# Modulation products by channel columns, and loads in another order, in a one-core mixer kernel

## The chip, the cores and the metric

The kernel runs on one core of a Trainium2 chip. A time is the device time of one launch in microseconds. The profiles show the engines of that core: PE (matrix products; PEld is its weight load), DVE, ACT and POOL (elementwise work), and SP, whose queue issues nearly all DMA transfers.

## The reference, cut to what matters

S = 2048 tokens, D = 640 channels, F = 1728; all in float32.

```python
mod = (silu(c) @ w_mod).reshape(1, 6, 1, D)         # w_mod: 640 x 3840
sa, ca, ga, sb, cb, gb = mod[:, 0], ..., mod[:, 5]
h = layernorm(x) * (1 + ca) + sa                    # x is q
x = x + ga * A(h, k, v, shift_k, ssm_k, ssm_D)
h = layernorm(x) * (1 + cb) + sb
x = x + gb * mixer_mlp(h, w1, b1, w2, b2)

def A(q, k, v, ...):
    kv = causal_conv_of_4_taps(k, shift_k) * v
    y = irfft(rfft(kv, 2 * S) * rfft(ssm_k, 2 * S))[:S] + kv * ssm_D
    return q * y                                    # per channel
```

## The kernel before

The operator A runs in five stages of 128 channels (the loop `for c in range(NC)`); a token MLP follows it. In a stage the long convolution is two small Fourier steps forward, a product, and two back:

- `step1(side, t)` is the first step, on PE, in four blocks t of 16 products; side 0 is kv (tile `X`, read with a stride), side 1 is ssm_k (tile `P`). ACT evacuates each block into `Z` (line 232).
- `f2(g)`, g = 0 to 7, is the second step (line 246), with the weights `W2`. ACT evacuates half of it to `KT` (line 250), DVE makes two products into `P` (`mul`), POOL adds them into `Y`, the tile `T_y` (`add`).
- `i2(r)`, r = 0 and 1, is the first step back (line 275, evacuated at 283 into part of `Z`), `i1(half)` the second (line 294, weights `V1`, the inverse's constant `c_v1`).
- `gate(c, ps, half)`: DVE multiplies by A1, the normalised and scaled q, and POOL adds to x. A1 is made by sixteen ACT operations `ac` (line 301, they need the statistics of the rows of q) and by DVE's scalings `po` with the rows G1 and G0.

The loop is software-pipelined. While stage c runs f2, i2 and i1, `step1` of stage c + 1 is woven in, and DVE fills its gaps (`dv(n)` takes n operations from the list `fill`) with the short convolution `kv_ops` of the stage after that, eight operations for each of four groups of rows. Group 2 is done by POOL for stages 0, 1 and 2. `kv_loads` and `load_k`, `load_v`, `load_halo` bring K and V in pieces of 128 KB, each issued on SP as soon as its group's last reader is issued.

Engines take their instructions in the order in which the program gives them (`manual_schedule`), so the order of the statements is the order on each engine and on SP's queue. A transfer waits on SP for the readers of the place that it overwrites, and all later transfers wait behind it; it also waits for the eighth transfer before it. Three PSUM buffers go around for PE's results (`psum`); the fourth, `tap`, holds DVE's kv work (`SV`, `TAP`).

What the change touches, in the order of time:

- The weights W2 are laid out by ACT: `lay_w2(i, n)` (line 110) copies quarter n of half i from a load `load_w2c(i)` in the tile `xb`. Half 0 is loaded before stage 1's K and V (line 481), half 1 behind them (489). The four lays of half 0 stand between the blocks of `step1(0, t)` of stage 0.
- q is loaded in 32 transfers (`load_q`, at f2's g = 3), into `xa` and `xb`, the second where the halves of W2 came in. Behind it come w_mod's blocks of 128 rows and 1920 columns, five of them (`mod_load`), into `T_v1`, `T_aux` and `P`.
- Statistics of q: DVE's `bn_stats` after f2 of stage 0 (lines 561, 562). `rstd` makes the reciprocal root from them: a root on ACT (338), an addition on POOL (339), four operations of DVE.
- Modulation of the first half of `mod`: `mod_part` (line 354) multiplies silu(c) with a block of w_mod, five parts of six products of 320 columns; `mod_sum` (358) evacuates; `mod_row(i)` (365) spreads row i over the partitions, and ACT and DVE make G0 and G1 of all 640 columns (372 to 377). They stand around `i2` of stage 0.
- The inverse's constant lands in `T_v1` where two w_mod blocks were, so it waits for `mod_part` 0 and 1. `load_ks(1)`, ssm_k of stage 1, lands in the first half of `T_aux` and waits for `mod_part` 2. Then come stage 2's K and V.
- `perm_add` and `perm` (line 176) bring ssm_k into `P`, which `step1(1, t)` reads behind i1.

Of the kernel before, what the change touches and what calls it, by code (L numbers as in the profile page):

```python
# [50 lines left out]
def mixer_kernel(ctx: ExitStack, tc: tile.TileContext, q, k, v, shift_k, ssm_k, ssm_D, w1, b1, w2, b2, c,  # L51
# [129 lines left out]

        act.activation(TAP, TR.rearrange("p (i s) -> p s i", s=4), AF.Copy)

    def kv_ops(g, eng=dve):
        S_, T_, W_ = (SV, TV, TAP) if eng is dve else (PS_.rearrange("p (n i) -> p n i", i=64),
                                                       PT.rearrange("p (n i) -> p n i", i=64), PW)
        w = lambda s: W_[:, None, s, :].to_broadcast([128, 8, 64])
        kx = lambda s: KX[:, 8 * g + 3 - s:8 * g + 11 - s, :]
        ops = [lambda: TT(eng, S_, kx(3), w(3), ALU.mult)]
        for s in (2, 1, 0):  # L190
            ops.append(lambda s=s: TT(eng, T_, kx(s), w(s), ALU.mult))
            ops.append(lambda: TT(eng, S_, S_, T_, ALU.add))
        ops.append(lambda: TT(eng, X.rearrange("p (n i) -> p n i", i=64)[:, 8 * g:8 * g + 8], S_,
                              VX[:, 8 * g:8 * g + 8], ALU.mult))
        return ops

# [22 lines left out]
        return ops  # L219


    def step1(side, t, later=False):

        ps = psum()
        for a in range(8):
            i = 8 * t + a
            lhs = KSP[:, i] if side else X.rearrange("p (m i) -> p i m", i=32)[:, i]
            o = 512 * (a % 2) + 128 * (a // 2)
            for ri in range(2):
                pe.matmul(ps[64 * ri:64 * ri + 64, o:o + 128], lhs, F1[:, 128 * ri:128 * ri + 128], start=True,  # L230
                          stop=True)
        evac = lambda: act.activation(Z[:, side, t].rearrange("p a k e -> p e a k"),  # L232
                                      ps.rearrange("p (e a k) -> p e a k", a=8, e=2), AF.Copy)
        return evac if later else evac()
# [126 lines left out]
    def mod_row(i, t, slot=None, later=False):  # L361

        ps, j = psum(slot).rearrange("p (h m) -> p h m", h=2), i % 3
        for h in range(2):
            pe.matmul(ps[:, h, 0:320], ones[32 * j:32 * j + 1, 0:1].to_broadcast([1, 128]),
                      t[32 * j:32 * j + 1, 320 * h:320 * h + 320], start=True, stop=True)
# [4 lines left out]
        if i == 0:  # L371
            act.activation(two(G0), ps, AF.Copy)
        elif i == 1:
            act.activation(two(G1), ps, AF.Copy, bias=1.0)
        elif i == 2:
            TT(dve, two(G0), ps, two(G0), ALU.mult)
            TT(dve, two(G1), ps, two(G1), ALU.mult)
        elif i == 3:
            act.activation(two(SB), ps, AF.Copy, accum_out=msb)
        elif i == 4:  # L380
            dve.tensor_scalar(two(CB), ps, 1.0, None, op0=ALU.add)


    NF, NW = 14, 2
    FS = (4, 5, 6, 7, 8, 9, 10, 11, 12)
# [87 lines left out]
    def run(ops):  # L473
        for f_ in ops:
            f_()
# [1 line left out]

    all_taps()
    load_taps(1, act)
    run(kv_ops(2, pool))  # L480
    load_w2c(0)
    run(kv_ops(0))
    kv_loads(1, 0)
    run(kv_ops(1))
    kv_loads(1, 1)
    kv_loads(1, 2)
    run(kv_ops(3))
    kv_loads(1, 3)
    load_w2c(1)
    for h in range(2):  # L490
        sync.dma_start(stg[7 * h:7 * h + 6, :], dram(b1, 864 * h, [[128, 6], [1, 128]]))
# [3 lines left out]
    perm_add(0)  # L495
    perm(0)
    all_taps()
    load_taps(2)
    for t in range(4):
        step1(0, t)  # L500
        lay_w2(0, t)
    run(kv_ops(2, pool))
    run(kv_ops(0))
    run(kv_ops(1))
    for t in range(4):
        step1(1, t)


    three = lambda t: [t[:, 640 * j:640 * j + 640] for j in range(3)]
    pl = [three(t) for t in (T_v1, T_v1[:, 1920:3840], T_aux, T_aux[:, 2048:3968], P)]  # L510

    def load_q():
        for j in range(16):
            for b in range(2):
                sync.dma_start(XH[j // 8][64 * b:64 * b + 64, j % 8], dram(q, (16 * b + j) * D, [[32 * D, 64], [1, D]]))
        for kk in range(4):
            mod_load(0, kk, (T_v1[:, 0:1920], T_v1[:, 1920:3840], T_aux[:, 0:1920], T_aux[:, 2048:3968])[kk])

    fill = kv_ops(3)

# [5 lines left out]
    for c in range(NC):  # L526
# [3 lines left out]
        for g in range(8):  # L530
            m_, a_ = f2(g)
            if pend_m:
                pend_m()
            if pend_a:
                pend_a()
            pend_a, pend_m = (pend_m and pa_next), m_
            pa_next = a_
            if c:
                for f_ in ac[2 * g:2 * g + 2]:
                    f_()  # L540
            if cn is None and g < 4:
# [23 lines left out]
            if c + 3 < NC:  # L565
                load_taps(c + 3)
        if c == 0:
            mod_load(0, 4, P[:, 0:1920])
            for t in range(4):
                step1(0, t)  # L570
            ps = psum()
            pe.transpose(ps[:, 0:36], stg, ID[0:36, 0:36])
            act.activation(cols, ps[:, 0:36], AF.Copy)
            act.activation(sil, cols[:, 30:35], AF.Silu)
            i2(0)
            for kk in range(4):
                mod_part(tap, kk, pl[kk])
                if kk == 1:
                    sync.dma_start(T_v1[:, 0:4096], c_v1, max_dma_last_dim=4096)
                if kk == 2:  # L580
                    load_ks(1)
            rstd(rs1, nm1, 0, 16)
            run(ac[0:4])
            i2(1)
            mod_part(tap, 4, pl[4])
# [12 lines left out]
            run(kv_ops(2, pool))  # L598
            for i in range(3):
                mod_row(i, T_kt[:, 0:640])  # L600
            taps()
            load_taps(3)
            perm_add(1, dve)
            perm(1)
            load_ks(2)
            run(ac[8:16])
            run(po[0:2])
            fill.extend(kv(3, ((0,), (1, 2), (3,))))
        elif cn is not None:
            for t in range(2):  # L610
                step1(0, t)
            perm(cn)
            if c + 2 < NC:
                fill.extend(kv(c + 3 if c + 3 < NC else None))
            else:
                fill.extend(x1s(cc, j) for cc in range(c) for j in range(16))
        else:
            blk.update({f: (j16(t[:, 0:2048]), j16(t[:, 2048:4096])) for f, t in (
                (0, mem("w0", 4096, "wb0")), (1, mem("w1", 4096, "wb1")))})
            mod_load(3, 3, T_z[:, 0:1920])  # L620
            mod_load(3, 4, P[:, 0:1920])
            for kk in range(3):
                mod_part(tap, kk, pl[kk])
            t = mem("in", 4288, "wb3")
            blk[3] = j16(t[:, 0:2048]), j16(t[:, 2048:4096])
            split_rows(0, X, (0, 1, 3))
            split_rows(1, T_aux[:, 0:2048], (0, 1, 3))
            run(po)
        if c:
# [25 lines left out]
        for half in range(2):  # L655
            ps = i1(half)
            if c and half:
                dv(3)
            elif c:
                k0 = step1(1, 0, True)  # L660
            elif half:
                run(po[2:4])
# [534 lines left out]
```

## Time and profile before

| | us |
|---|---|
| median of 3 runs | 704.31 (702.51 to 707.6) |
| the profiled execution | 706.67 |
| its span, first to last instruction | 704.6 |
| PE busy / weight load busy | 641.4 / 620.4 |
| DVE busy | 501.5 |
| ACT busy | 307.8 |
| POOL busy | 156.1 |

The busy shares are sums over stages with different limits. In the five stages PE, DVE and POOL hand work to each other, and a stage is read by which of them ends a wait last; the MLP after them is PE's. The rows that matter stand in the prediction. A timeline row gives start and duration in us, engine and line, tiles, and in brackets how long the engine was idle before and what ended it. A row of windows gives, behind each engine's busy time, PE's granted clock, the share of the DMA engines and GB/s.

### The profile page before, as it was taken

What the parts mean: (1) busy time and instruction counts of PE and PEld (TensorE: products, weight loads), DVE (VectorE), ACT (ScalarE), POOL (GpSimd) and SP (SyncE); (2) the same over time, 40 slices, a digit from 0 to 9 for tenths busy, and PEclk for the clock granted to TensorE, in tenths of its full rate; (3) what the DMA queues carried; (4) which work ended last, traced back from release to release, by engine and by line L of the source; (5) the groups of instructions that cost most, each with busy time, mean ns of one, the idle gap of its engine ahead of it and who ended that gap; (6) DMA issues with size and microseconds to landing.
All of it is one profiled execution on the core that took longest, in us unless ns stands there. A gap on an engine that the chain in (4) does not pass through costs nothing.

```text
span 704.6 us, 20705 instructions
## 1 busy us (share of the span) xinstructions
PE 641.4 (91%) x9078; PEld 620.4 (88%) x9078; DVE 501.5 (71%) x846; ACT 307.8 (44%) x463; POOL 156.1 (22%) x135
## 2 busy tenths in 40 slices
PE   0699769999999999978888999999999999999997
PEld 0699569989989989758878999999999999999997
DVE  7688578969878638679886430564377699888886
ACT  0664644635745545345766420431243332333331
POOL 5297058625527328100010000000000000000000
PEclk9999979999999899799999999999999999999999
DMA  9978978346433522334030833357385634555511
GB/s 182 213 217 263 325 159 176 86 78 143 78 68 92 151 56 70 114 83 98 1 60 22 158 62 59 78 130 160 112 234 152 205 116 128 153 170 171 155 52 39
DMA packets 170848, 89.36 MB, mean 127 GB/s; under 512 B 89571, under 2 KB 160518, under 8 KB 170758
## 3 DMA queue, kind: packets, MB, share of 16 engines
q1 hardware_dynamic: 166210, 86.73, 48.8%
q10 hardware_dynamic: 4548, 1.31, 1.1%
q8 instruction: 71, 1.16, 0.7%
q14 instruction: 19, 0.16, 0.1%
HBM read 74.25 MB, written 13.76 MB: 125 GB/s over the span
## 4 chain that ended last, share of the span: by engine, by line
PE 67%; DVE 14%; DMA 6%; POOL 5%; ACT 4%; issue 3%; SPq 0%; ACTq 0%; DVEq 0%; POOLq 0%
PE pst L1059 20%; PE pst L446 17%; PE pst L246 8%; PE pst L230 7%; PE pst L275 6%; POOL y L60 4%; PE pst L1123 4%; PE pst L947 3%; DMA aux<-in_A_ssm_k_dram 3%; PE pst L294 2%; DVE aux L60 2%; DVE tap L60 1%; DVE p L60 1%; PE tap L354 1%; DVE kt L60 1%
## 5 line engine op out<-in xcount | busy, mean ns | idle before, releaser
L246 PEld LDWEIGHTS pst<-z,w 128*64 128x64 f32 x2560 | 94.7, 141 | 7.7 <-ACT z L232 7.3
L246 PE MATMUL pst<-z,w 128*64 128x64 f32 x2560 | 95.7, 240 | 6.2 <-ACT z L232 6.1
L60 POOL TENSOR_TENSOR y<-p 128x256 f32<-128x256 f32 x72 | 92.5, 1353 | 24.3 <-DVE p L60 23.9
L60 DVE TENSOR_TENSOR p<-pst,kt 128x512 f32<-128x512 f32 x80 | 52.6, 693 | 22.1 <-ACT kt L250 15.9
L230 PE MATMUL pst<-v,x 128*64 128x128 f32 x640 | 45.8, 304 | 23.2 <-POOL t L471 23.2
L232 ACT ACTIVATE z<-pst 128x1024 f32<-128x1024 f32 x40 | 45.8, 1144 | 43.9 <-PE pst L230 25.9
L230 PEld LDWEIGHTS pst<-v,x 128*64 128x64 f32 x640 | 43.8, 221 | 23.7 <-issue 23.2
L1059 PE MATMUL pst<-r_z,m_w 128*128 128x320 f32 x259 | 48.5, 309 | 1.3 <-DVE m_w L60 1.3
L275 PEld LDWEIGHTS pst<-v,y 32*128 32x128 f32 x1280 | 43.3, 210 | 6.5 <-POOL y L60 2.7
L275 PE MATMUL pst<-v,y 32*128 32x64 f32 x1280 | 45.3, 297 | 2.8 <-DVE y L60 2.1
L1047 ACT ACTIVATE m_w<-m_v 128x896 fp32r<-128x896 f32 x30 | 27.8, 948 | 42.6 <-DVE m_v L60 27.4
L230 PE MATMUL pst<-v,p 128*64 128x128 f32 x640 | 40.0, 284 | 7.0 <-DVE aux L60 4.9
L250 ACT ACTIVATE kt<-pst 128x512 f32<-128x512 f32 x40 | 25.2, 631 | 48.0 <-PE pst L246 25.6
L230 PEld LDWEIGHTS pst<-v,p 128*64 128x64 f32 x640 | 37.4, 143 | 8.3 <-DVE aux L60 5.1
L1059 PEld LDWEIGHTS pst<-r_z,m_w 128*128 128x128 f32 x259 | 40.6, 188 | 1.5 <-DVE m_w L60 1.5
L60 DVE TENSOR_TENSOR m_w<-m_v,m_w 128x896 fp32r<-128x896 f32 x30 | 32.5, 1087 | 11.2 <-ACT m_w L1047 11.2
L853 ACT ACTIVATE pst<-pst,sm 128x640 f32<-128x640 f32 x14 | 10.7, 767 | 59.3 <-PE pst L446 59.3
L60 DVE TENSOR_TENSOR tap<-tap,kt 128x512 f32<-128x512 f32 x51 | 35.6, 698 | 1.3
L60 DVE TENSOR_TENSOR kt<-in,tap 128x512 f32<-128x512 f32 x51 | 35.1, 688 | 1.5
L1059 PE MATMUL pst<-h_x,m_w 128*128 128x320 f32 x168 | 33.7, 309 | 0.0
L283 ACT ACTIVATE z<-pst 128x512 f32<-128x512 f32 x38 | 21.4, 665 | 27.9 <-PE pst L275 27.9
L1047 ACT ACTIVATE m_w<-m_p 128x896 fp32r<-128x896 f32 x13 | 12.4, 954 | 44.5 <-DVE m_p L60 27.6
(310 smaller groups left out, 1395.6 us busy)
## 6 DMA issues: line engine op xcount, KB each, us to landing
x<-in_B_w_dram SPq DMA_DIRECT2D x20, 512.0 KB
m_v<-in_B_w_dram SPq DMA_DIRECT2D x19, 384.0 KB
aux<-in_A_ssm_k_dram SPq DMA_DIRECT2D x10, 512.0 KB
m_x<-xs SPq DMA_DIRECT2D x32, 160.0 KB
out_dram<-m_x SPq DMA_DIRECT2D x32, 160.0 KB
in<-in_A_k_dram SPq DMA_DIRECT2D x36, 128.0 KB
in<-in_A_v_dram SPq DMA_DIRECT2D x36, 128.0 KB
x<-in_B_w_dram SPq DMA_DIRECT2D x10, 384.0 KB
```

The lines of the kernel that those rows point to most:

```text
L60: TT = lambda eng, o, a, b, op: eng.tensor_tensor(o, a, b, op=op)
L230: pe.matmul(ps[64 * ri:64 * ri + 64, o:o + 128], lhs, F1[:, 128 * ri:128 * ri + 128], start=True, stop=True)
L232: evac = lambda: act.activation(Z[:, side, t].rearrange("p a k e -> p e a k"), ps.rearrange("p (e a k) -> p e a k", a=8, e=2), AF.Copy)
L246: pe.matmul(ps[64 * h:64 * h + 64, o:o + 64], W2[k1 // 32][:, 2 * (k1 % 32) + ri], rhs, start=True, stop=True)
L250: act.activation(kt.rearrange("p (m i) -> p m i", i=32), pv[:, :, 1], AF.Copy)
L275: pe.matmul(pp[qd // 2][:, o:o + 64], Y[p, ri, i:i + 2].rearrange("p i k -> p (i k)"), V2[p, 64 * ri:64 * ri + 64], start=ri == 0, stop=ri ...
L283: act.activation(o, i, AF.Copy)
L446: pe.matmul(ps[0:m, h, 0:320], w_.bitcast(F32R), r_[:, 320 * h:320 * h + 320].bitcast(F32R), start=first and i == 0, stop=last and i == 2)
L947: pe.matmul(ps[n][:, h, 0:320], sets[n][:, j].bitcast(F32R), r[:, 320 * h:320 * h + 320].bitcast(F32R), start=j == 0 and r is hh, stop=j = ...
L1047: act.activation(W[n][0].bitcast(F32R), A[p, w_], AF.Copy)
L1059: pe.matmul(bank[n], w[:, i].bitcast(F32R), r.bitcast(F32R), start=i == 0 and k == 0, stop=i == 6 and k == 2)
L1123: pe.matmul(acc[s][:, h, 0:320], w[:, f_].bitcast(F32R), u[r + h].bitcast(F32R), start=f_ == 0 and k == 0, stop=f_ == NF - 1 and k == 2)
```

## The change

1. Stage 0's kv goes to the first half of `T_y` instead of `X` (the arguments `x` of `kv_ops` and `step1`).
2. `load_w2c(0)` moves behind the loads of K and V of stage 1, and the four lays of half 0 move from `step1(0, t)` to `step1(1, t)`.
3. q comes in pairs of rows, 16 transfers; its first half is issued before stage 0's `step1`, its second at g = 3. Behind that the inverse's constant and ssm_k of stage 1 are issued at once, then stage 2's K and V.
4. w_mod's first half is taken by columns of channels, all 640 rows at a time: 128 columns (stage 0) are loaded behind q's first half into `T_aux`, 256 (stages 1 and 2) after `i2` of stage 0 into `T_y`, 256 (stages 3 and 4) after `i2` of stage 1, again into `T_y`. `cols_part` makes 15 products, `cols_rows` spreads three rows and makes that part of G0 and G1. The first runs before `i2` of stage 0; the others run between the blocks of `step1(1, t)` at the ends of stages 0 and 1, and DVE's part of them stands ahead of the kv operations there.
5. The transpose of the staged rows and silu(c) move into f2 of stage 0 (g = 5).
6. In stage 0, POOL's scaling of the taps, `perm_add(1)` (now on POOL) and stage 2's group 2 of `kv_ops` move ahead of `rstd`; `perm(1)` stands behind `ac[8:16]` and all four scalings.

```diff
-    def kv_ops(g, eng=dve):
+    def kv_ops(g, eng=dve, x=X):
...
-    def step1(side, t, later=False):
+    def step1(side, t, later=False, x=X):
...
+    def cols_load(place, c0, n):
+        for kk in range(5):
+            sync.dma_start(place[:, 3 * n * kk:3 * n * kk + 3 * n].rearrange("p (j m) -> p j m", j=3),
+                           dram(w_mod, 128 * kk * 6 * D + c0, [[6 * D, 128], [D, 3], [1, n]]))
+    def cols_part(place, n, slot=None):
+        ps = psum(slot)
+        for kk in range(5):
+            for j in range(3):
+                o = n * (3 * kk + j)
+                pe.matmul(ps[32 * j:32 * j + 32, 0:n], sil[:, kk:kk + 1].to_broadcast([128, 32]), place[:, o:o + n],
+                          start=kk == 0, stop=kk == 4)
+        act.activation(T_kt[0:96, 0:n], ps[0:96, 0:n], AF.Copy)
+    def cols_rows(c0, n):
+        for i in range(3):
+            ps, g0, g1 = psum()[:, 0:n], G0[:, c0:c0 + n], G1[:, c0:c0 + n]
+            pe.matmul(ps, ones[32 * i:32 * i + 1, 0:1].to_broadcast([1, 128]), T_kt[32 * i:32 * i + 1, 0:n], ...)
+            if i == 0:
+                act.activation(g0, ps, AF.Copy)
+            elif i == 1:
+                act.activation(g1, ps, AF.Copy, bias=1.0)
+            else:
+                TT(dve, g0, ps, g0, ALU.mult)
+                TT(dve, g1, ps, g1, ALU.mult)
...
-    run(kv_ops(2, pool))
-    load_w2c(0)
-    run(kv_ops(0))
+    x0 = T_y[:, 0:2048]
+    run(kv_ops(2, pool, x0))
+    run(kv_ops(0, dve, x0))
     kv_loads(1, 0)
-    run(kv_ops(1))
+    run(kv_ops(1, dve, x0))
     kv_loads(1, 1)
     kv_loads(1, 2)
-    run(kv_ops(3))
+    run(kv_ops(3, dve, x0))
     kv_loads(1, 3)
+    load_w2c(0)
     load_w2c(1)
...
+    M0, M1 = T_aux[:, 2048:3968], T_y[:, 0:3840]
+    def load_q(half):
+        for j in range(0, 8, 2):
+            for b in range(2):
+                sync.dma_start(XH[half][64 * b:64 * b + 64, j:j + 2],
+                               dram(q, (16 * b + 8 * half + j) * D, [[32 * D, 64], [D, 2], [1, D]]))
+    load_q(0)
+    cols_load(M0, 0, 128)
     load_taps(2)
     for t in range(4):
-        step1(0, t)
+        step1(0, t, x=x0)
+    for t in range(4):
+        step1(1, t)
         lay_w2(0, t)
     run(kv_ops(2, pool))
     run(kv_ops(0))
     run(kv_ops(1))
-    for t in range(4):
-        step1(1, t)
...
                 if g == 3:
-                    load_q()
+                    load_q(1)
+                    sync.dma_start(T_v1[:, 0:4096], c_v1, max_dma_last_dim=4096)
+                    load_ks(1)
+            if c == 0 and g == 5:
+                (transpose of stg, cols, sil, as before)
...
         if c == 0:
-            (mod_load 4, step1(0, t), transpose, i2(0), mod_part 0 to 3 with the loads of c_v1 and ssm_k,
-             rstd, ac[0:4], i2(1), mod_part 4)
             (K and V of stage 2)
-            mod_sum(tap, T_kt[:, 0:640])
-            run(ac[4:8])
             pool.tensor_scalar(PW, TR.rearrange("p (i s) -> p s i", s=4), 1.0, None, op0=ALU.mult)
+            perm_add(1)
+            for t in range(4):
+                step1(0, t)
             run(kv_ops(2, pool))
-            for i in range(3):
-                mod_row(i, T_kt[:, 0:640])
+            cols_part(M0, 128)
+            i2(0)
+            cols_rows(0, 128)
+            rstd(rs1, nm1, 0, 16)
+            run(ac[0:8])
+            i2(1)
+            run(po[0:2])
+            cols_load(M1, 128, 256)
+            run(ac[8:16])
+            run(po[2:4])
+            perm(1)
             taps()
             load_taps(3)
-            perm_add(1, dve)
-            perm(1)
             load_ks(2)
-            run(ac[8:16])
-            run(po[0:2])
...
             i2(1)
+            if c == 1:
+                cols_load(M1, 384, 256)
             step1(0, 3)
...
         for t in range(1 if c else 0, 4):
             step1(1, t)
+            if t == (1 if c == 0 else 2) and c < 2:
+                cols_part(M1, 256)
+                cols_rows(128 + 256 * c, 256)
```

More of the change, by code (lines that the diff above doesn't have):

```diff
@@ L192, in kv_ops @@
             ops.append(lambda: TT(eng, S_, S_, T_, ALU.add))
-        ops.append(lambda: TT(eng, X.rearrange("p (n i) -> p n i", i=64)[:, 8 * g:8 * g + 8], S_,
+        ops.append(lambda: TT(eng, x.rearrange("p (n i) -> p n i", i=64)[:, 8 * g:8 * g + 8], S_,
                               VX[:, 8 * g:8 * g + 8], ALU.mult))
@@ L226, in step1 @@
             i = 8 * t + a
-            lhs = KSP[:, i] if side else X.rearrange("p (m i) -> p i m", i=32)[:, i]
+            lhs = KSP[:, i] if side else x.rearrange("p (m i) -> p i m", i=32)[:, i]
             o = 512 * (a % 2) + 128 * (a // 2)
@@ L370, in mod_row @@
             return lambda: act.activation(two(GB), ps, AF.Copy)
[L371 to L378, printed above, removed]
+        if i == 3:
             act.activation(two(SB), ps, AF.Copy, accum_out=msb)
@@ L381, in mod_row @@
             dve.tensor_scalar(two(CB), ps, 1.0, None, op0=ALU.add)
+    def cols_load(place, c0, n):
[13 more added lines that the diff above has]
+            ps, g0, g1 = psum()[:, 0:n], G0[:, c0:c0 + n], G1[:, c0:c0 + n]
+            pe.matmul(ps, ones[32 * i:32 * i + 1, 0:1].to_broadcast([1, 128]), T_kt[32 * i:32 * i + 1, 0:n], start=True,
+                      stop=True)
+            if i == 0:
[5 more added lines that the diff above has]
+                TT(dve, g1, ps, g1, ALU.mult)
     NF, NW = 14, 2
@@ L497, in mixer_kernel @@
     all_taps()
+    three = lambda t: [t[:, 640 * j:640 * j + 640] for j in range(3)]
+    M0, M1 = T_aux[:, 2048:3968], T_y[:, 0:3840]
[6 more added lines that the diff above has]
+    cols_load(M0, 0, 128)
     load_taps(2)
     for t in range(4):
-        step1(0, t)
+        step1(0, t, x=x0)
+    for t in range(4):
+        step1(1, t)
         lay_w2(0, t)
@@ L504, in mixer_kernel @@
     run(kv_ops(1))
-    for t in range(4):
-        step1(1, t)
[L509 to L517, printed above, removed]
     fill = kv_ops(3)
@@ L549, in mixer_kernel @@
                 if g == 3:
-                    load_q()
+                    load_q(1)
+                    sync.dma_start(T_v1[:, 0:4096], c_v1, max_dma_last_dim=4096)
+                    load_ks(1)
+            if c == 0 and g == 5:
+                ps = psum()
+                pe.transpose(ps[:, 0:36], stg, ID[0:36, 0:36])
+                act.activation(cols, ps[:, 0:36], AF.Copy)
+                act.activation(sil, cols[:, 30:35], AF.Silu)
             dv(-(-len(fill) // max(6 - g, 1)))
@@ L567, in mixer_kernel @@
         if c == 0:
[L568 to L585, printed above, removed]
             load_k(2, 1)
@@ L660, in mixer_kernel @@
                 k0 = step1(1, 0, True)
-            elif half:
-                run(po[2:4])
             gate(c, ps, half)
```

## The prediction

> **What bounds the kernel now.** The page first, then the chain of waits that ended last in order of time, for the stretch that the change touches (stage 0 and 1, up to 190 us).
>
> ```profile
> span 704.6 us, 20705 instructions
> ```
>
> ```profile
> 76.50 0.64 SPq L164
> 77.19 14.79 DMA aux<-in_A_ssm_k_dram
> ...
> 102.25 1.24 DVE aux L60
> 103.53 5.93 PE pst L230 x64
> ...
> 110.63 14.37 PE pst L246 x377
> ...
> 135.06 3.58 PE pst L275 x120
> ...
> 155.19 1.23 DVE aux L60
> 156.42 0.60 DVE kt L60
> ...
> 165.67 1.27 DVE p L60 x2
> ...
> 172.50 10.28 POOL y L60 x8
> ...
> 185.95 3.58 PE pst L275 x120
> ```
>
> Two different limits. In stage 0's tail the late thing is ssm_k of stage 1: its SP issue waits for the modulation products (they read the place it lands in), it lands at 92, and perm, ac[8:16], the scalings, the gate and the last two step1 blocks follow; stage 1's f2 starts at 110.63. In stage 1's tail the chain leaves PE at the second gate (155.19) and runs through DVE: kv operations one after another from 156.42, then the first product of f2 (165.67), then POOL's y additions without a gap, then i2 at 185.95. So a wait put on DVE between 156.42 and 165.67 moves stage 2's i2 one for one. After 190 us nothing is edited.
>
> **The change part by part.**
>
> (1) Start: both halves of the w2 constant now stand behind stage 1's K and V loads. Timeline and SP's waits:
>
> ```profile
> 16.34 3.51 SPq L104 DMA_DIRECT2D xb<-in_const_w_dram  x1
> ...
> 19.97 1.27 SPq L150 DMA_DIRECT2D in<-in_A_v_dram  x2
> ...
> 33.81 0.63 SPq L104 DMA_DIRECT2D xb<-in_const_w_dram  x1
> ...
> 33.84 1.17 ACT L110 ACTIVATE w<-xb,v 128x1024 f32<-128x1024 f32 x1
> ...
> 36.81 3.25 SPq L160 DMA_DIRECT2D rows<-in_A_shift_k_dram  x2
> ...
> 39.72 1.10 ACT L232 ACTIVATE z<-pst 128x1024 f32<-128x1024 f32 x1 [0.61 <-PE pst L230]
> ...
> 40.87 18.98 PE L246 MATMUL pst<-z,w 128*64 128x64 f32 x511 [1.19 <-ACT z L232]
> ```
>
> ```profile
> SPq L160 <- DMA xb<-in_const_w_dram: 2.2, 1, 2.2
> ```
>
> The half issued at 33.81 released the second taps load after a wait of 2.2, so it landed near 36.81 + 3.25 - 0.5 = 39.5, 5.7 after its issue. Stage 1's K/V issues take 19.97 to 33.81. Without the 1 MB ahead of them I let them end 2.3 earlier, so the first half is issued at 31.5 and lands at 37.2. The 3.5 at 16.34 I take for the queue full of ssm_k's small pieces, which the next load inherits. ACT now does lay, evacuate, lay, evacuate behind that landing; f2 needs three lays and three evacuations: 3 x (1.17 + 1.10) = 6.8, so f2 starts at 44.0, **3.1 later**. Bounds: 0 (lays hidden as now) and, landing no earlier than today's second half, 39.5 + 6.8 - 40.9 = 5.4. The kv products into the other place start earlier; POOL and DVE wait for f2 anyway: nothing gained.
>
> (2) Stage 0's tail. Rows:
>
> ```profile
> 51.12 1.24 ACT L110 ACTIVATE w<-xb,v 128x1024 f32<-128x1024 f32 x1
> ...
> 78.23 0.31 ACT L338 ACTIVATE sm<-sm 128x16 f32<-128x16 f32 x1 [1.88 <-DVE sm L562]
> ...
> 78.63 0.28 POOL L339 TENSOR_SCALAR sm<-sm 128x16 f32<-128x16 f32 x1 [12.88 <-ACT sm L338]
> ...
> 80.16 1.65 ACT L301 ACTIVATE aux<-xa,sm 128x128 f32<-128x128 f32 x4 [1.62 <-DVE sm L343]
> ...
> 82.67 2.17 ACT L283 ACTIVATE z<-pst 128x512 f32<-128x512 f32 x4 [0.87 <-PE pst L275]
> ...
> 87.59 5.75 PE L294 MATMUL pst<-z,v 64*64 64x64 f32 x256 [0.76 <-ACT g L372]
> ...
> 89.84 2.86 SPq L144 DMA_DIRECT2D in<-in_A_k_dram  x4
> ...
> 92.38 2.48 DVE L60 TENSOR_TENSOR aux<-aux,g 128x1024 f32<-128x1024 f32 x2
> ...
> 92.43 2.13 ACT L176 ACTIVATE p<-aux 128x2048 f32<-128x2048 f32 x1 [3.75 <-DMA in<-in_A_k_dram]
> ...
> 96.36 2.51 POOL L60 TENSOR_TENSOR t<-in,t 128x512 f32<-128x512 f32 x2 [16.28 <-DMA in<-in_A_k_dram]
> ...
> 102.50 1.31 SPq L150 DMA_DIRECT2D in<-in_A_v_dram  x2
> ...
> 113.89 1.29 DVE L60 TENSOR_TENSOR p<-pst,kt 128x512 f32<-128x512 f32 x2 [2.54 <-ACT kt L250]
> ```
>
> The ssm_k wait goes: it is now issued behind q's last rows and the inverse's constant, which wait for the last lay (51.12 + 1.24 = 52.4, now 55.5). What is late next? In POOL's new order rstd's addition (L339) stands behind eight kv operations of stage 2, and DVE's Newton step needs it. Their K/V loads stand on SP behind ssm_k: 76.50 to 89.84 = 13.3 today from ssm_k's issue to the first of them. Two q issues and the constant at 0.6 each bring ssm_k to 57.2, the K loads to 70.5, POOL's start 6.5 later (89.84 to 96.36) to 77.0, eight operations of 1.26 to 87.1, L339 to 87.4. From L339's end to ac took 80.16 - 78.91 = 1.25: ac starts at 88.6. The statistics alone would allow 78.23 + 3.1 + 2 = 83.4, the lower bound.
> From there ACT is serial: ac[0:8] 3.3, i2's evacuation 2.2 (to 94.1), ac[8:16] 3.3 (97.4), perm 2.1 (99.5). PE: i1 from 94.1 to 99.9, then two step1 blocks of 1.82 (the row of 155.06 below, three blocks) to 103.5. DVE: two scalings of 1.24 after 97.4, two gates of 1.24 to 102.4; the second block needs the first gate (101.1), so DVE is covered.
>
> (3) The column products, on the path twice:
>
> ```profile
> 77.63 1.28 PE L354 MATMUL tap<-aux,sm 128*32 128x320 f32 x12 [1.18 <-DMA aux<-in_w_mod_dram]
> ...
> 85.46 1.37 PE L365 MATMUL pst<-kt,sm 1*128 1x320 f32 x12 [1.61 <-ACT kt L358]
> ...
> 87.57 1.55 DVE L60 TENSOR_TENSOR g<-pst,g 128x640 f32<-128x640 f32 x2 [7.50 <-ACT g L372]
> ...
> 155.06 5.46 PE L230 MATMUL pst<-v,p 128*64 128x128 f32 x96
> ```
>
> The program's six calls show as twelve, so a call of 320 columns costs 0.213; fifteen of 256 cost 15 x 0.213 x 0.8 = 2.56 (half of it is the lower bound). Then one evacuation 0.6 with its waits, three rows 3 x 0.228 x 0.8 = 0.55, the last evacuation left over 0.3, DVE's two products 0.8 (0.78 each at 640 columns).
> *After stage 0:* 103.5 + 2.56 + 0.6 + 0.55 = 107.2; two step1 blocks and an evacuation (3.64 + 1.2) give f2 at 112.1 (+1.5). DVE's 11 kv operations of 0.71 (9.25 for the 13 from 156.42 to 165.67) end at 107.2 + 1.1 + 7.8 = 116.1 and its first product follows (+2.2 against 113.89). Between the two: **i2 at 137.1, +2.0**. With ac at 83.4 it is -3.2; with (1)'s upper bound and K/V two later still, +6.3.
> *After stage 1:* the two step1 blocks ahead of the products end at 155.06 + 2 x 1.82 = 158.7, and DVE, free at 156.42, stands at the row products: 2.3 + 2.56 + 0.6 + 0.55 + 0.3 + 0.8 = **7.1 later** for its 13 kv operations, for f2's first product, for POOL's chain and i2. Nothing covers it. Bounds 5.8 and 9.5 (transfer late).
>
> (4) The columns' transfers. Windows:
>
> ```profile
> 42.00:62.00 20.00, 20.00 (x525) 20.00 (x523) 14.20 (x23) 9.54 (x13) 19.84 (x16) 1.00 0.78 222
> 66.00:78.00 12.00, 10.18 (x203) 7.39 (x203) 11.59 (x37) 7.33 (x10) 0.00 (x0) 1.00 1.02 394
> 103.00:110.00 7.00, 5.90 (x64) 5.66 (x64) 6.69 (x11) 1.63 (x2) 6.69 (x6) 0.64 0.95 180
> ```
>
> 256 columns are 1.97 MB: 5.0 us at w_mod's 394 GB/s, 8.9 at q's 222. In stage 0 they follow stage 2's K/V, whose issues take 89.84 to 103.81 = 14.0, so 84.5 plus three, landing by 97 while PE comes at 103.5: hidden by 6. In stage 1 they are issued at i2's end (near 147) and land by 159 at worst; PE comes at 160.7. Rows of q in pairs, 32 issues less 16, only feed loads that wait for the last lay: nothing.
>
> [...]
>
> (5) Sum: 2.0 + 7.1 = 9.1. The profiled execution took 706.67, its span 704.6 and 2.07 around it: 713.7 and 715.8. It lies 2.4 above the median of the runs shown, 704.31; on the median the sum is 713.4.
>
> **The rivals.**
> *A, not slower: the transfers run ahead.* Place: SP's queue up to stage 2's K/V. If the constant lands early enough to hide the lays and POOL has done its kv operations before the statistics end, ac starts at 80.2, 8.4 before the main case: i2 of stage 1 at -6.4, and +7.1 makes 705.0. Deciding point: L339 before 79. For it: half the q issues, no w_mod block of 4.9 MB ahead. Against: the last lay at 55.6 and 13.3 of ssm_k still lie ahead of those loads.
> *B, slower still: the columns come late.* If SP stands longer at ssm_k, the first 256 columns land after 104; each us later is one us more. A landing at 108.5 makes 718.4. Against: 6 us of cover.
> *C, faster:* A, and DVE's wait in stage 1 costs nothing, since POOL's additions had slack that I don't see: 704.3 - 6.4 = 697.9, a little less with the clock kept up (5.93 against 3.64). Against: POOL's eight additions at 172.50 stand in the chain without a gap.
>
> **How the numbers follow.** Main case 0.58 (713.4, its own range 709 to 718), A 0.22 (705.0), B 0.12 (718.4), C 0.08 (697). One per cent, 7 us, is about what a measurement of this kernel can tell from no change. Above 711.3: B and 0.83 of the main case, 0.60. Faster than 697.3: C, 0.08. Between: 0.32. The range 704 to 719 leaves out C and the outer parts of B and the main case.
>
> **What would show it.** Right: f2 of stage 0 starting 2 to 4 later; L339 on POOL well after the statistics, behind kv operations, and ac after it; an idle stretch of some 6 us on DVE behind stage 1's second gate, ended by PE; stage 2's i2 some 9 later. Wrong: L339 before 80, or f2's first product of stage 2 not later than stage 1's shift.

## The result and the profile after

The changed kernel takes 725.32 us (median of 4, 721.41 to 728.4), the kernel before 703.57 beside it (median of 4): ratio 1.032, 95% interval 1.0276 to 1.0363. The forecast was 713.4. The direction is right, the size is not: 21.75 more instead of 9.1. Ratios here and below leave out disturbed executions, medians don't, so the two can differ by a few tenths of a per cent.

The chain of waits of the changed kernel (its profiled execution: 726.19, span 724.1), in order of time; start, duration, what:

```profile
43.74 8.46 PE pst L246 x221
52.20 4.20 issue x2
...
56.54 6.92 DMA xb<-in_A_q_dram
63.48 14.72 SPq L164
...
83.01 3.49 DMA in<-in_A_k_dram
...
86.66 2.50 POOL t L60 x2
...
96.09 5.70 DMA y<-in_w_mod_dram
...
103.48 5.81 PE pst L294 x256
...
146.52 3.58 PE pst L275 x120
...
191.39 10.13 POOL y L60 x8
...
204.74 5.04 PE pst L275 x120
```

i2 of stage 1 stood at 135.06 before and stands at 146.52: 11.5 later, where 2.0 was forecast. i2 of stage 2 stood at 185.95 and stands at 204.74: 18.8 later, so stage 1's tail costs 7.3, where 7.1 was forecast. Another 0.7 comes behind it: the profiled executions lie 19.5 apart, the medians 21.75. Nearly the whole miss lies in stage 0's tail.

The rows of that tail in the timeline of the changed kernel, and behind the last "..." three of stage 1's tail. Lines have moved: L389 is `cols_part`, L397 and L400 are `cols_rows`; L164 is still ssm_k, L144 K, L301 `ac`.

```profile
54.86 6.04 PE L246 MATMUL pst<-z,w 128*64 128x64 f32 x162 [2.66 <-issue]
62.05 16.16 SPq L164 DMA_DIRECT2D aux<-in_A_ssm_k_dram  x2
67.83 2.29 PE L246 MATMUL pst<-z,w 128*64 128x64 f32 x38 [3.33 <-issue]
80.97 2.67 SPq L144 DMA_DIRECT2D in<-in_A_k_dram  x4
88.36 0.31 ACT L338 ACTIVATE sm<-sm 128x16 f32<-128x16 f32 x1
97.30 0.27 POOL L339 TENSOR_SCALAR sm<-sm 128x16 f32<-128x16 f32 x1
98.24 3.18 ACT L301 ACTIVATE aux<-xa,sm 128x128 f32<-128x128 f32 x8 [9.57 <-DVE sm L343]
...
112.86 2.36 PE L389 MATMUL pst<-y,sm 128*32 128x256 f32 x30
116.86 0.76 DVE L60 TENSOR_TENSOR g<-pst,g 128x256 f32<-128x256 f32 x2 [5.57 <-ACT g L400]
121.83 5.37 PE L246 MATMUL pst<-z,w 128*64 128x64 f32 x140 [1.24 <-ACT z L232]
125.40 1.28 DVE L60 TENSOR_TENSOR p<-pst,kt 128x512 f32<-128x512 f32 x2
...
167.22 1.23 DVE L60 TENSOR_TENSOR aux<-pst,aux 128x1024 f32<-128x1024 f32 x1 [3.34 <-PE pst L294]
174.75 0.76 DVE L60 TENSOR_TENSOR g<-pst,g 128x256 f32<-128x256 f32 x2 [6.30 <-ACT g L400]
184.75 1.28 DVE L60 TENSOR_TENSOR p<-pst,kt 128x512 f32<-128x512 f32 x2
```

Two things are to be seen. First, the chain that the prediction drew is there, but 10 later: K's loads leave SP at 80.97 (forecast 70.5), POOL starts at 86.66 (77.0), the addition L339 comes at 97.30 (87.4) and `ac` at 98.24 (88.6). From `ac` on everything in this tail keeps its forecast distance within 0.7. Second, something the prediction did not have: inside f2 of stage 0 PE stands still twice (2.66 and 3.33) with no releaser: the weight loads that end the stops, at 54.86 and 67.83, wait for no semaphore. In the DMA view of those stretches all 16 engines are full: the packets of the queue q1 take 110.0% of their span from 51.8 to 55.2 and 100.1% from 64.6 to 67.8. The first row below is from the windows of the changed kernel (the last three numbers: PE's clock, DMA share, GB/s), the other two from its DMA view from 51.8 to 55.2:

```profile
50.00:58.00 8.00, 5.34 (x148) 5.21 (x145) 4.21 (x8) 3.71 (x5) 4.98 (x6) 1.00 1.06 247
...
q1 hardware_dynamic: 1543, 0.84, 110.0%
q8 instruction: 1, 0.02, 2.5%
```

One packet of kind "instruction", 16 KB, is served in that stretch; its record starts at 52.20, when PE's first run of products ends, and PE goes on at 54.86. A second one starts at 65.10, in the other stretch. The trace lets one count PE's records (products, weight loads and waits for semaphores). When these two packets were served, 961 and 1473 of them had started. In all runs below with such stops in this f2, the stops come at 961, 1217 or 1473 (within 1), so 256 apart, and at no other place. The packet between the two was served at 56.98, when 1084 had started, and PE did not stop at 1217. With q by single rows, in the kernel before and in the first experiment, the packets come some 180 to 240 records before PE reaches these places. That PE waits for its own program in these stretches is the author's reading of these counts; the trace names no releaser.

### The profile page after: what moved, and what is told of

The parts are those of the page before. It is cut to its first block, busy times and chain, and to the rows that moved or that the text cites. A ratio compares the mean times of both kernels' runs of the same rounds, so it can differ in the third digit from the quotient of the medians.

```text
span 724.1 us, 20801 instructions
## 1 busy us (share of the span) xinstructions
PE 649.6 (90%) x9114; PEld 629.9 (87%) x9114; DVE 498.2 (69%) x848; ACT 308.6 (43%) x469; POOL 151.8 (21%) x137
## 4 chain that ended last, share of the span: by engine, by line
PE 59%; DVE 14%; DMA 6%; issue 6%; POOL 6%; ACT 5%; SPq 3%; ACTq 0%; DVEq 0%; POOLq 0%
PE pst L1082 19%; PE pst L469 17%; PE pst L275 5%; POOL y L60 4%; PE pst L230 4%; PE pst L246 4%; PE pst L1146 3%; PE pst L970 3%; PE pst L294 3%; DVE tap L60 2%; SPq L164 2%; DVE kt L60 2%; DMA in<-in_A_k_dram 1%; POOL t L60 1%; DVE p L60 1%
## 5 line engine op out<-in xcount | busy, mean ns | idle before, releaser
L246 PE MATMUL pst<-z,w 128*64 128x64 f32 x2560 | 97.3, 241 | 15.1 <-ACT z L232 7.7
L60 POOL TENSOR_TENSOR y<-p 128x256 f32<-128x256 f32 x72 | 89.8, 1294 | 55.2 <-DVE p L60 54.9
L230 PE MATMUL pst<-v,p 128*64 128x128 f32 x640 | 37.4, 274 | 2.4 <-issue 1.5
L230 PE MATMUL pst<-v,x 128*64 128x128 f32 x512 | 39.3, 316 | 0.0
L230 PEld LDWEIGHTS pst<-v,p 128*64 128x64 f32 x640 | 35.0, 137 | 3.8 <-ACT g L400 1.7
L230 PEld LDWEIGHTS pst<-v,x 128*64 128x64 f32 x512 | 37.2, 221 | 0.7
L294 PEld LDWEIGHTS pst<-z,v 64*64 64x64 f32 x1280 | 22.7, 149 | 13.0 <-ACT z L283 9.9
L294 PE MATMUL pst<-z,v 64*64 64x64 f32 x1280 | 24.2, 234 | 10.0 <-ACT z L283 9.3
```

The lines of the kernel that those rows point to most:

```text
L60: TT = lambda eng, o, a, b, op: eng.tensor_tensor(o, a, b, op=op)
L246: pe.matmul(ps[64 * h:64 * h + 64, o:o + 64], W2[k1 // 32][:, 2 * (k1 % 32) + ri], rhs, start=True, stop=True)
L294: pe.matmul(ps[64 * b:64 * b + 64, 512 * e + 64 * jj:512 * e + 64 * jj + 64], V1[p, ri, n2], T2[p, :, 32 * ri + n2], start=ri == 0, stop=r ...
```

## The experiments

Theories: T1, pairs of rows of q fill the DMA engines, so that what shares them comes late; T2, the order alone, ssm_k ahead of K and V on SP; T3, rstd's addition on POOL; T4, DVE's wait for the columns in stage 1's tail. Every ratio is to the kernel before on the same chip (702.31, 701.26, 703.07 and 703.15 in the four sets); the changed kernel's is 1.032.

**q by single rows again.**

```diff
-        for j in range(0, 8, 2):
+        for j in range(8):
             for b in range(2):
-                sync.dma_start(XH[half][64 * b:64 * b + 64, j:j + 2], ...[[32 * D, 64], [D, 2], [1, D]])
+                sync.dma_start(XH[half][64 * b:64 * b + 64, j], ...[[32 * D, 64], [1, D]])
```

> The changed kernel with q loaded again row by row (32 transfers instead of 16), the order unchanged. T1 (pairs of rows fill all DMA engines without moving more bytes a second, and what shares the engines comes late): TensorE's two idle stretches inside the first stage's f2 that end at 54.9 and 67.8 without a releaser (2.7 and 3.3 us) go, statistics begin near 66 instead of 72.2, the constant and ssm_k land earlier, and ac[0:8] starts at 89 to 92 instead of 98.2: 716 to 719. T2 (the order alone: ssm_k and the constant behind q; its 128-byte pieces hold SP for 14.7 us whatever q looks like): K loads for stage 2 still start near 81, ac near 98, and 16 more issues of 0.6 only add: 725 to 730.

724.45, ratio 1.0326 (1.0248 to 1.0405): no gain. Timeline rows, and one of the windows, of this kernel:

```profile
44.01 15.25 PE L246 MATMUL pst<-z,w 128*64 128x64 f32 x384 [4.04 <-ACT z L232]
81.44 2.75 SPq L144 DMA_DIRECT2D in<-in_A_k_dram  x3
98.11 0.27 POOL L339 TENSOR_SCALAR sm<-sm 128x16 f32<-128x16 f32 x1
99.06 3.18 ACT L301 ACTIVATE aux<-xa,sm 128x128 f32<-128x128 f32 x8 [16.35 <-DVE sm L343]
...
50.00:58.00 8.00, 8.00 (x224) 8.00 (x221) 6.68 (x12) 5.82 (x7) 8.00 (x7) 1.00 0.81 219
```

Half of T1 holds: PE's stretches are gone, at a DMA share of 0.81 instead of 1.06 and at 219 GB/s instead of 247. The other half falls: K's loads still leave at 81.44, because twice as many q issues hold SP instead (13.59 and 12.01 for the two halves, from 37.83 and 56.28, where the pairs took 7.94 and 5.57). `ac` now waits 16.35 for DVE's step behind POOL's addition. The 6 us that PE won are under that wait.

**q over all 128 partitions.** One transfer takes the same pair of rows of both halves of the partitions, 8 transfers instead of 16.

```diff
-            for b in range(2):
-                sync.dma_start(XH[half][64 * b:64 * b + 64, j:j + 2], ...[[32 * D, 64], [D, 2], [1, D]])
+            sync.dma_start(XH[half][:, j:j + 2], ...[[16 * D, 2], [32 * D, 64], [1, 2 * D]])
```

> The changed kernel with q's pairs of rows taken over all 128 partitions by one transfer (8 transfers instead of 16, pieces as long as before). T1a (64 partitions at a time are what holds q at 225 GB/s; w_mod over 128 runs at 394): each half of q takes 6 to 7 us instead of 11 to 12, the idle stretches of TensorE shrink with it, ssm_k follows 5 to 8 earlier and ac starts near 90: 715 to 719. T1b (the length of the pieces or their place in DRAM holds q): same rate, same idle stretches: 724 to 727. T2 (order alone): as T1b.

801.21, ratio 1.1405 (1.1336 to 1.1474): neither. SP's row and a window of this kernel:

```profile
38.18 24.10 SPq L527 DMA_DIRECT2D xa<-in_A_q_dram  x4
...
40.00:60.00 20.00, 16.21 (x400) 15.84 (x397) 10.14 (x16) 13.18 (x16) 12.09 (x10) 0.91 0.14 54
```

The DMA engines are busy to 0.14, at 54 GB/s; in the DMA view of the same stretch the queue q1, for which the view lists q's issues alone, takes 12.5% of the 16 engines' span, as much as two of them. The outermost dimension of the source is 2 here; whether that is the reason was not tried by itself. Whether 64 partitions at a time are what holds q near 225 GB/s this run can't tell. It shows one thing besides: f2 of stage 0 runs here without a stop (15.40 from 44.34), with pairs of rows, but with the engines at 0.14. So in this f2 the stops go with the full engines, not with the pairs as such.

**Epsilon on DVE.** Only the engine of L339 is changed.

```diff
-        pool.tensor_scalar(v_, v_, EPS, None, op0=ALU.add)
+        dve.tensor_scalar(v_, v_, EPS, None, op0=ALU.add)
```

> The changed kernel with rstd's addition of epsilon on VectorE instead of GpSimd, where it stands behind eight kv operations. T3 (this one instruction holds ac from 90 to 98.2): ac[0:8] starts at 89.5 to 90.5, everything behind it in this stage 7 to 8 earlier: 716.5 to 719. Rival (T2: late K/V loads hold stage 2's kv products anyway, so VectorE's first product of the second stage stays near 124): 723 to 726.

719.55, ratio 1.0238 (1.0165 to 1.031), 5 to 6 less than the changed kernel. Its timeline:

```profile
89.98 0.61 DVE L339 TENSOR_SCALAR sm<-sm 128x16 f32<-128x16 f32 x1
93.56 3.19 ACT L301 ACTIVATE aux<-xa,sm 128x128 f32<-128x128 f32 x8 [3.60 <-DVE sm L343]
```

T3 holds, a little smaller than expected: `ac` comes at 93.56 instead of 98.24. The statistics end 1.3 later in this run, and two of the small operations of DVE behind L339 took 1.15 and 1.13 there (0.19 and 0.18 in the changed kernel; why is not shown), so it isn't the 90 of the expectation.

**The gates' products on POOL.**

```diff
-                TT(dve, g0, ps, g0, ALU.mult)
-                TT(dve, g1, ps, g1, ALU.mult)
+                ga = T_rows[:, 256:256 + n]
+                act.activation(ga, ps, AF.Copy)
+                TT(pool, g0, ga, g0, ALU.mult)
+                TT(pool, g1, ga, g1, ALU.mult)
```

> The changed kernel in which ScalarE evacuates the third row of the column products into a free place and GpSimd makes the two products with the gates, so that VectorE does not stand at them. T4 (VectorE's wait of 6.3 and 0.76 of products behind the second stage's second gate is the price of the columns there): first product of the third stage's f2 near 178 instead of 184.75, 718 to 719. Rival (GpSimd, which makes the y additions of the third stage, or the evacuations on ScalarE, take the time up): 722 to 726.

723.52, ratio 1.0297 (1.0222 to 1.0373): the rival's figure, and by its time alone not to be told from the changed kernel (1.0276 to 1.0363). Its timeline at stage 1's end:

```profile
167.82 1.22 DVE L60 TENSOR_TENSOR aux<-pst,aux 128x1024 f32<-128x1024 f32 x1 [4.46 <-PE pst L294]
178.58 19.05 PE L246 MATMUL pst<-z,w 128*64 128x64 f32 x512 [1.24 <-ACT z L232]
181.99 1.29 DVE L60 TENSOR_TENSOR p<-pst,kt 128x512 f32<-128x512 f32 x2 [3.63 <-ACT kt L250]
```

From the second gate to the first product of stage 2: 10.5 before (155.19 to 165.67), 17.5 in the changed kernel (167.22 to 184.75), 14.2 here. DVE's wait is gone, and only half of the 7 comes back: PE, which carries the column products and waits twice for ACT's evacuations between them (0.49 at 174.21 and 0.46 at 175.37), is next, and f2's evacuation ends DVE's wait.

**The first half of w2 early.** Load and lays where the kernel before has them.

```diff
     run(kv_ops(2, pool, x0))
+    load_w2c(0)
     run(kv_ops(0, dve, x0))
...
     for t in range(4):
         step1(0, t, x=x0)
+        lay_w2(0, t)
     for t in range(4):
         step1(1, t)
-        lay_w2(0, t)
```

> The changed kernel with the first half of the w2 constant loaded, and laid out, where the kernel before does it. The prediction's first term (f2 of the first stage 3 later): f2 starts near 41 instead of 43.7 and, since ssm_k waits for the last lay and K/V stand behind it, 2 to 3 come back: 722 to 723.5. Rival (other transfers are pushed back by the same 1 MB, so the K loads of stage 2 still go out near 81): 724.5 to 726.

725.19, ratio 1.0327 (1.0277 to 1.0376): the rival. f2 starts 1.8 earlier, K's loads do not:

```profile
41.91 8.45 PE L246 MATMUL pst<-z,w 128*64 128x64 f32 x222 [1.19 <-ACT z L232]
81.95 3.43 SPq L144 DMA_DIRECT2D in<-in_A_k_dram  x4
99.54 3.18 ACT L301 ACTIVATE aux<-xa,sm 128x128 f32<-128x128 f32 x8 [11.46 <-DVE sm L343]
```

**ssm_k behind K and V.** `load_ks(1)` moves behind stage 2's K and V on SP, `perm_add(1)` behind rstd's addition on POOL; epsilon stays on POOL.

```diff
                     sync.dma_start(T_v1[:, 0:4096], c_v1, max_dma_last_dim=4096)
-                    load_ks(1)
...
             load_v(2, 3)
+            load_ks(1)
...
-            perm_add(1)
...
             rstd(rs1, nm1, 0, 16)
+            perm_add(1)
```

> The changed kernel with ssm_k of the second stage issued behind the K and V loads of the third instead of ahead of them, and its small addition behind rstd's on GpSimd; epsilon stays on GpSimd. T2 (the late K/V loads, behind ssm_k's 16 on SP, are what makes GpSimd's kv operations and so rstd's addition late): first K load near 63 instead of 81, the eight kv operations done before the statistics end, ac[0:8] at 89.5 to 91 instead of 98.2: 716.5 to 719. Rival (GpSimd is late for another reason, or ssm_k now lands after 104 and perm takes the place of the wait): 722 to 727.

721.14, ratio 1.027 (1.021 to 1.033). The mechanism came as T2 has it, the time came half:

```profile
62.56 11.58 SPq L144 DMA_DIRECT2D in<-in_A_k_dram  x4
89.78 0.28 POOL L339 TENSOR_SCALAR sm<-sm 128x16 f32<-128x16 f32 x1
90.73 3.19 ACT L301 ACTIVATE aux<-xa,sm 128x128 f32<-128x128 f32 x8 [3.32 <-DVE sm L343]
...
102.29 1.39 PE L294 MATMUL pst<-z,v 64*64 64x64 f32 x79 [1.65 <-issue]
```

So K's late loads made POOL late, and POOL's addition made `ac` late: two different cures of one chain bring `ac` to 93.6 and 90.7. The times of the two are less sharp than the rows: their intervals overlap with that of the changed kernel. f2 of stage 1 starts 5.4 earlier here (116.40). Most of the rest of the 7.5 went in i1, which takes 7.7 (95.98 to 103.68) instead of 5.81: PE stops once more without a releaser, 1280 records, five times 256, behind its last stop in f2.

**Single rows and epsilon on DVE together.**

> The changed kernel with both q row by row and epsilon's addition on VectorE. With q by rows alone TensorE reached the end of the first stage 6 earlier, but ac stayed at 98 to 99 behind GpSimd; with the addition alone ac came at 93.6, behind the statistics. If both delays are real and the first was only covered by the second, ac starts at 83 to 85 and the two come back together, 13 to 15 off the first i2 of the second stage, less what the late K/V loads then hold: 711 to 714. If the idle stretches of TensorE under paired rows were no cost of their own, no better than the addition alone: 718 to 720.

717.72, ratio 1.0223 (1.0167 to 1.0279): `ac` comes when expected, the time doesn't. The timeline:

```profile
83.51 3.19 ACT L301 ACTIVATE aux<-xa,sm 128x128 f32<-128x128 f32 x8 [1.45 <-DVE sm L343]
...
103.61 0.63 PE L389 MATMUL pst<-y,sm 128*32 128x256 f32 x6 [0.75 <-DMA y<-in_w_mod_dram]
104.30 0.38 ACT L391 ACTIVATE kt<-pst 96x256 f32<-96x256 f32 x1 [4.10 <-PE pst L389]
...
106.33 6.31 PE L230 MATMUL pst<-v,p 128*64 128x128 f32 x64 [0.45 <-ACT g L400]
```

With `ac` 15 earlier, PE reaches the 256 columns before they have landed, and their products, 2.36 in one piece in the changed kernel, take from 98.98 to 104.2. That is the wait that the prediction's rival B names; it was hidden as long as `ac` was late. It is 2.9 of the some 7 that are missing: f2 of stage 1 starts 8 earlier, not 15. Behind the wait, the 64 products of two step1 blocks take 6.31 (3.71 for the two blocks ahead of it, at 95.28), and i1 takes 6.60 instead of 5.81.

**All mendings together.** Single rows, epsilon on DVE, w2 early, the later gates' products on POOL, and:

```diff
-            if t == (1 if c == 0 else 2) and c < 2:
+            if t == 2 and c < 2:
                 cols_part(M1, 256)
-                cols_rows(128 + 256 * c, 256)
+        if c < 2:
+            cols_rows(128 + 256 * c, 256)
```

> All mendings together: q by rows, epsilon on VectorE, the first half of w2 early, the products with the gates for the later columns on GpSimd from a row that ScalarE evacuates, and TensorE's small row products moved behind the last step1 block so that it doesn't wait for the evacuation. By the terms found so far: 14 from the first stage's tail, 2.5 from w2, 4 to 5 from the second stage's tail, out of 22: 700 to 704. If the column products still hold TensorE (2.4 and 0.7 in each tail) and nothing hides them: 704 to 708.

707.0, ratio 1.008 (1.0046 to 1.0113), in the second range of the expectation. What is left in stage 0's tail is again the columns, PE's row at 104.02 in this kernel's timeline, and f2 behind it:

```profile
104.02 0.68 PE L389 MATMUL pst<-y,sm 128*32 128x256 f32 x6 [0.20 <-DMA y<-in_w_mod_dram]
...
109.71 14.35 PE L246 MATMUL pst<-z,w 128*64 128x64 f32 x384
```

**The columns ahead of DVE's K and V.** As the kernel with all mendings, with this order on SP at stage 0's end:

```diff
             load_halo(2)
-            load_k(2, 0)
-            load_v(2, 0)
-            load_v(2, 1)
-            load_k(2, 3)
-            load_v(2, 3)
...
             cols_load(M1, 128, 256)
+            load_k(2, 0)
+            load_v(2, 0)
+            load_v(2, 1)
+            load_k(2, 3)
+            load_v(2, 3)
```

> All mendings together, and the 256 columns for the first stage's tail put on SP ahead of the K and V loads of VectorE's groups instead of behind them. In the run with all mendings TensorE stood 3 us at these columns' transfers (idle stretches released by y from w_mod) and ran their products between 97.5 and 106, instead of 2.4 us in one piece. If that is what is left of the first stage's tail, f2 of the second stage starts near 105 instead of 109.7 and the time is 701.5 to 704. If the K/V loads behind them now hold VectorE's kv operations: 705 to 709.

705.56, ratio 1.0007 (0.9967 to 1.0047): no difference from the kernel before. (The medians, 705.56 and 703.07, lie 0.35% apart.) PE's timeline and the chain:

```profile
106.80 14.38 PE L246 MATMUL pst<-z,w 128*64 128x64 f32 x384
...
185.89 3.58 PE pst L275 x120
```

f2 of stage 1 starts at 106.80, not the 105 of the expectation, but 3.8 earlier than before (110.63), and stage 1's tail gives it back: i2 of stage 2 at 185.89, before 185.95. No version here beats the kernel before.

**The same, with q in pairs; and the kernel before with q in pairs alone.**

> The kernel with all mendings and the columns ahead of K/V, with q again by pairs of rows. Nothing covers the end of the first stage's statistics there. If pairs of rows stop TensorE (two idle stretches of 2.7 and 3.3 us in f2 whose releaser the profile doesn't show, while all 16 DMA engines are full): 5 to 7 slower than the same kernel with single rows. If the stretches have another reason, or the fewer issues make up for them: within 2 of it.

> The kernel before with one thing of the change: q by pairs of rows (16 transfers instead of 32). There q is loaded behind the last lay, from 56 us on, with the w_mod blocks behind it. If pairs fill the DMA engines at the same rate and stop TensorE for it: the first products of modulation 2 to 4 later, 703 to 706 beside 701 to 704 before. If the price of pairs is only that of the place where the change loads them, ahead of f2: no difference within 1.

The mended kernel with pairs: 711.43, ratio 1.0109 (1.0073 to 1.0146), by the ratios 1.0% or 7 above its twin with single rows, as expected. The kernel before with pairs: 711.89, ratio 1.012 (1.0063 to 1.0176), more than was expected. PE in the first, then in the second:

```profile
53.54 7.01 PE L246 MATMUL pst<-z,w 128*64 128x64 f32 x162 [2.76 <-issue]
```

```profile
60.77 5.86 PE L246 MATMUL pst<-z,w 128*64 128x64 f32 x127 [3.66 <-issue]
69.03 2.19 PE L246 MATMUL pst<-z,w 128*64 128x64 f32 x36 [2.41 <-issue]
```

So pairs of rows cost 1% in these kernels, in which nothing covers the end of the statistics.

**Pairs of rows that are not neighbours.** As few transfers, but pieces of 2560 bytes as with single rows:

```diff
-        for j in range(0, 8, 2):
+        for j in range(4):
             for b in range(2):
-                sync.dma_start(XH[half][64 * b:64 * b + 64, j:j + 2], ...[[32 * D, 64], [D, 2], [1, D]])
+                sync.dma_start(XH[half][64 * b:64 * b + 64, j:j + 5:4], ...[[32 * D, 64], [4 * D, 2], [1, D]])
```

> The kernel with all mendings and the columns ahead of K/V, with q by pairs of rows that don't lie side by side (rows j and j + 4 in one transfer): as few transfers as with neighbouring pairs, and as much handed over by each, but pieces of 2560 bytes as with single rows. If the backlog stops TensorE (half as many issues hand over the same bytes faster than the engines move them, and instructions queue behind): all engines full, the same two idle stretches of 2 to 3 us in f2, as slow as neighbouring pairs, 709 to 712. If the long pieces of 5120 bytes do it: no idle stretches, as fast as single rows, 702 to 706.

711.74, ratio 1.0129 (1.0075 to 1.0183), with the same stretches of PE. Its timeline and windows:

```profile
53.47 7.08 PE L246 MATMUL pst<-z,w 128*64 128x64 f32 x162 [2.77 <-issue]
...
50.00:58.00 8.00, 5.23 (x116) 5.08 (x114) 3.54 (x6) 3.04 (x4) 4.29 (x5) 0.79 1.10 245
```

It is not the length of the pieces. What pairs change is how much SP has handed over ahead of the engines. Where SP waits for nothing, an issue takes 0.64 us for a single row and for a pair alike (in the first experiment from 41.49, in the changed kernel from 41.70): 0.164 MB in 0.64 is 256 GB/s, 0.328 MB is 512, and the engines move 203 to 251 in these windows. With pairs SP soon waits for the eighth transfer before (from the columns' fourth issue on in the changed kernel, 47.92 and 49.35), so up to eight pairs, 2.6 MB, lie ahead of whatever comes next; eight single rows are 1.3 MB. That PE's instructions come late behind such a pile is the author's estimate: the runs leave the pile as the reason, since neither the length of the pieces nor the number of bytes is; its height was not varied by itself, and how it would hold up a packet of instructions is not shown.

## Why the prediction was wrong, by its steps

1. *Start, f2 3.1 later:* right. f2 of stage 0 starts at 43.74, forecast 44.0. But these 3 do not carry on into stage 0's tail as the sum had it: with w2 early, K's loads and `ac` stayed where they were.
2. *Stage 0's tail, `ac` at 88.6:* the step that failed, by 9.6; i2's 11.5 lies outside the bounds given for it (-3.2 to +6.3). Its chain, ssm_k, K, POOL, L339, `ac`, is the right one, as the two cures show; two of its terms were too small. "Two q issues and the constant at 0.6 each" brought ssm_k to 57.2. It left at 62.05, 4.9 later, since all eight issues of q's second half stood behind the taps load on SP, which left at 55.2, and not only the last two. And the 13.3 from ssm_k to K, taken from the kernel before, became 18.9 (62.05 to 80.97), 5.6 more. ssm_k holds SP for 16.2 of it; the same two transfers hold it for 9.6 with q by single rows, and for 4.1 where they go behind K and V. As far as these three show, the time goes with what lies ahead of ssm_k, and the kernel before had other loads ahead of it. The other terms came nearly right (K to POOL 5.7 for 6.5, POOL's operations 10.6 for 10.4). With single rows the two terms are 68.97 and 12.5, with the same sum. What was missing in the sum is bytes. An estimate made afterwards: q 5.24 MB, the first columns 0.98, the constant 2.10 and ssm_k 1.05 stand ahead of K; 9.4 MB at q's 222 GB/s is 42 us, and from 37.55, where q starts, that is 80, against 79 to 83 for K's first issue in all runs with this order on SP and q to 64 partitions, in pairs or single rows. The 222 is a mean over a busy stretch, so this can't be better than a few us; and it says when the bytes have moved, not when a load leaves SP: with ssm_k behind K, K's first load left at 62.56, and POOL could start on it only at 79.13. The row of 222 GB/s was quoted in the prediction, and used for the columns alone.
3. *Column products:* right. 2.36 for the fifteen products (forecast 2.56), DVE's wait of 6.30 and 0.76 in stage 1's tail, 7.3 in all for 7.1, within its bounds. "Nothing covers it" needs a correction: PE's columns alone hold the tail for half of it when DVE is freed.
4. *Transfers hidden:* right for the columns, in part by luck: PE's products at 112.86 wait for no transfer, but the columns landed near 102 (96.09 and 5.70 in the chain), not by 97, and PE came 9 later than forecast. With `ac` at its forecast there would have been some 2 of cover (an estimate from these rows), not 6. Wrong for the pairs of rows of q, put at "nothing". In the changed kernel itself they do cost nothing, since taking them back saved nothing; but only because `ac` waits for POOL. The price without that cover is 7 to 9, by the ratios of three kernels (the mended one with either kind of pairs, and the one before with pairs).
5. *Clock:* no extra price on the chain. i1 takes 5.81 at a granted clock of 0.64 (103.4 to 109.3), 5.75 before at 0.71 (87.6 to 93.4). The 64 step1 products behind it take 3.71 at 1.00 (109.3 to 112.9); before, 64 took 5.93 at 0.64. Rival C takes off "a little" for a clock kept up: these products took 2.2 less at 1.00, and what moves the clock is not shown.
6. *Rivals:* A needed L339 before 79; it came at 97.30. B's condition, SP standing longer at ssm_k, came true, but the columns landed near 102, not after 104, and PE came only at 112.86, so that they were in time; the wait that B names showed itself once `ac` was early. C did not occur.

## What to carry to other kernels

When loads are queued ahead of something, add up their bytes over the rate that the same kind of load shows in the trace, and not only the issues: in these runs the last load of such a queue did not land before about that time, with q in pairs or single rows. When it leaves the issuing queue is another matter. A tiny operation that is put behind a long list on another engine inherits everything that the list waits for: L339, 0.27 of work, came at 97.30 behind POOL's eight operations, and at 89.98 on DVE. And undoing one part of a change tells its price only where nothing else covers it: single rows saved nothing in the changed kernel and 1% in the mended one.

## What the hardware showed that was not expected

- PE stood still while the DMA engines were full: stretches of 0.95 to 3.83 us, two or three each, without a releaser in f2 of stage 0 of every kernel that loaded q in pairs to 64 partitions, at a DMA share of 0.97 to 1.11, and none there with single rows at 0.70 to 0.92. They lie 256 or 512 of PE's records apart, and in the changed kernel a packet of 16 KB of kind "instruction" is served in each (from 52.20 and 65.10). That PE waits for its program there is the author's reading. Four more, of 1.13 to 1.65, stood later in stage 0's tail, one of them in a kernel with single rows (1.43 before 97.92, with the columns ahead of K and V); their price is not known.
- q over all 128 partitions, in transfers whose outermost dimension is 2, ran at a DMA share of 0.14 and 54 GB/s (40 to 60); its queue took 12.5% of the 16 engines' span there, as much as two of them. What sets that share is not shown. That kernel was 14% slower than the kernel before, and 10% slower than the changed kernel (801.21 against 725.32), from which it differs in this alone.
- While q is loaded to 64 partitions at a time and the engines are full, 216 to 231 GB/s move in the windows 42 to 50 and 58 to 66 of the changed kernel and of the mended one with either kind of pairs, with pieces of 2560 and of 5120 bytes. What holds it there no run here shows.
